# Four row blocks of W3 as halves, and batch 0 ahead of the last block: reordering the loads and the first stage of a fused retention and feed-forward kernel

## Chip, cores and metric

The kernel runs on one core of one Trainium2 chip, alone. The metric is device time in microseconds (us) of one execution. The kernel before takes 182.81 us, the median of three executions between 182.58 and 183.25. The profile is of a further execution of the same program, whose span from first to last instruction is 183.3 us; times inside it are counted from the span's start.

## What is computed

Two stages stand one behind the other. The first is a retention layer, given as a recurrence over 768 positions for 4 batches and 8 heads of width 64. The second is a feed-forward layer with a product of two projections in place of an activation.

```python
# retention: q, k, v are [4, 8, 768, 64] in float32
gamma = 1.0 - 2.0 ** (-5.0 - np.arange(H))
for t in range(S):
    state = gamma * state + outer(k[:, :, t], v[:, :, t])
    y[:, :, t] = (1 / sqrt(D)) * (q[:, :, t] @ state)
x = y.transpose(0, 2, 1, 3).reshape(B * S, H * D)      # [3072, 512]

# feed-forward: w1, w2 [512, 1024], w3 [1024, 1024], w_out [1024, 512]
h = ((x @ w1) * (x @ w2)) @ w3
out = h @ w_out                                        # [3072, 512]
```

There is nothing between the last two products, so `w3 @ w_out` can be multiplied out once, as a matrix of 1024 x 512, and each token then needs one product in place of two. The kernel does this at its start; the change is about that start.

## The kernel before, in words

**Instructions are issued in written order.** The scheduler is set to manual, so each engine executes its instructions in the order in which the Python code calls them. An instruction that waits holds up everything behind it on its own engine, and nothing on the others. There are six queues to keep in mind: TensorE (PE, with its weight loads PEld), VectorE (DVE), ScalarE (ACT), GpSimd (POOL), and SyncE (SP), from which the loads are issued by `dma_in` (line 63).

**Loads.** Every input comes in float32 into a ring of 22 staging tiles of 128 x 1024 (`new_stage`, tile name `stg`). A row block of W3, W1 or W2 is 128 rows of 4 KB (`load_rows`), a block of w_out is 128 pairs of rows (`load_wo`), and the first two chunks of q, k and v of a batch are 128 x 8 pieces of 512 bytes (`load_pairs`). All go through one queue, in this order: W3 block 0, w_out block 0, W3 1, w_out 1, W3 2, w_out 2, W3 3, w_out 3; then W3 blocks 4 to 7; then q, k, v of batch 0 and of batch 1; then W1 and W2 (four blocks each); then later chunks of q, k and v. Each of the tiles is 512 KB.

**W3 times w_out.** `W3O[f]` (f = 0 to 7) is row block f of the product. W3 block f is cast to float16 (`cast_w3`), turned by eight 128 x 128 transposes on PE (`w3_transpose`, lines 240 to 248), copied from the accumulator memory (PSUM) to `w3t[f]`, and multiplied with the eight half blocks of w_out (`WO`, cast by `cast_wo`), eight matmuls of 512 columns that add up in one PSUM bank. For blocks 0 to 3 these eight are taken in four parts of two matmuls (`w3_part(f, i)`, line 255, with i the w_out block), because w_out arrives in turn with W3; four banks are held as `acc`. Blocks 4 to 7 go through `W3Block` (line 269), whose `mm(n)` issues the next n of the eight matmuls and whose `back` copies the result out on ACT (line 276). `busy(m, n)` (line 686) issues m matmuls of n columns on zeros, whose result nobody reads; they fill time on PE.

**First batches.** `Pairs(e)` (e = 0, 1) handles the first 256 positions of batch e: casts of q, k, v, transposes of q and k, `scores`, `intra` (scores times v), `kv` (the state), `inter` (state times q), and `outputs_back` to `XT[e]`, the input of the feed-forward layer. In `v_cast` on POOL, v is scaled with decays; `YS` holds the output decays, made in `output_decays` by three multiplications on DVE and three exponentials on ACT; `masks_and_decays` makes masks and constants on POOL.

**Start of the feed-forward layer.** `by_rows(W1, ps, d, blocks)` (line 795) multiplies row block d of W1 with the first tokens; there is one group of matmuls per block d, since the blocks arrive one by one. The first of them waits for the first half cast of W1 block 0 on ACT (line 769) and, for the columns from 512 on, on POOL (line 770). The end of batch 1's retention stands between these groups. After that one step follows another for each pair of chunks, in which PE has work all the time: the feed-forward products (`Ffn.mm`, line 636, and `o_unit`, line 663) of one pair of chunks and the retention of the next.

Of the kernel before, what the change touches and what calls it, by code (L numbers as in the profile page):

```python
# [10 lines left out]
HP = mybir.dt.float16  # L11
# [7 lines left out]
def kernel(  # L19
# [11 lines left out]
    nc = tc.nc  # L31
# [39 lines left out]
    def load_q(n):  # L71

        g, e = divmod(n, 2)
        if g >= NSTEP // 2:
            return
        bp, cp = divmod(g, NCH // 2)
        q_in[n] = load_pairs(q, bp * 2 + e, cp)

    def load_pairs(src, b, cp):
        t = new_stage()  # L80
        dma_in(
            t[:, :].rearrange("p (h x) -> p h x", x=2 * D),
            src[b, :, cp * 2 * C : (cp + 1) * 2 * C, :].rearrange("h (p t) d -> p h (t d)", t=2),
        )
        return t
# [19 lines left out]
    def new_stage():  # L105
        return wstage.tile([128, 1024], FP, tag="wst", name="stg")

    def load_rows(src, i):
        t = new_stage()
        dma_in(t[:, :], src[i * 128 : (i + 1) * 128, :])  # L110
        return t

    def load_wo(i):
        t = new_stage()
        dma_in(
            t[:, :].rearrange("p (t n) -> p t n", t=2),
            moe_w_out[i * 256 : (i + 1) * 256, :].rearrange("(p t) n -> p t n", t=2),
        )
        return t

    w3_st, wo_st = [], []
    for i in range(4):
        w3_st.append(load_rows(moe_w3, i))
        wo_st.append(load_wo(i))
    for f in range(4, 8):
        w3_st.append(load_rows(moe_w3, f))
    for e in range(2):
        load_q(e)
        k_in[e] = load_pairs(k, e, 0)
        v_in[e] = load_pairs(v, e, 0)  # L130
    w1_st = [load_rows(moe_w1, d) for d in range(4)]
    w2_st = [load_rows(moe_w2, d) for d in range(4)]
    load_q(2)
# [36 lines left out]
    keep = const.tile([128, L], FP, name="keep")  # L170
    keep_t = const.tile([128, 2, 128], FP, name="keep_t")

    def masks_and_decays():

        nc.gpsimd.memset(keep[:, :], 1.0)
        for s in range(2):
            r = slice(s * L, (s + 1) * L)
            nc.gpsimd.affine_select(
                out=keep[r, :], in_=keep[r, :], compare_op=mybir.AluOpType.is_ge, fill=0.0,
                base=0, pattern=[[1, 2], [2, 32]], channel_multiplier=-1,  # L180
            )

        nc.gpsimd.memset(keep_t[:, :, :], 1.0)
        for s in range(2):
            for t in range(2):
                nc.gpsimd.affine_select(
                    out=keep_t[half(s), t, :], in_=keep_t[half(s), t, :], compare_op=mybir.AluOpType.is_ge,
                    fill=0.0, base=-t, pattern=[[1, 2], [2, 64]], channel_multiplier=-2,
                )
        for h in range(H):  # L190
            for s in range(2):
                nc.gpsimd.memset(LGP[half((h + s) % 2), s, h // 2 : h // 2 + 1], math.log(gam[h]))
        for h in range(H):
            p, r = h // 2, (h % 2) * 64
            nc.gpsimd.memset(GS[r : r + 64, p : p + 1], gam[h] ** C)

    def output_decays():
        for n, (s, swap) in enumerate(((0, 0), (1, 0), (1, 1))):
            x = fsb.tile([128, NP, L], FP, tag="pa", name="ys_x", bufs=8)
            nc.vector.tensor_tensor(  # L200
                x[:, :, :], if_f[:, s, :].unsqueeze(1).broadcast_to((128, NP, L)),
                LGP[:, swap, :].unsqueeze(2).broadcast_to((128, NP, L)), MULT,
            )
            nc.scalar.activation(YS[:, n, :, :], x[:, :, :], AF.Exp)

    mark_t = const.tile([1, 1], HP, name="mark")
    XT = {}
# [8 lines left out]
    def cast_to(dst, src, on_dve):  # L216
        if on_dve:
            nc.vector.tensor_copy(dst, src)
        else:
            nc.scalar.copy(dst, src)  # L220

    def cast_wo(i):
        dst = WO[i][:, :, :].rearrange("p a n -> p (a n)")
        nc.scalar.copy(dst[:, 0:512], wo_st[i][:, 0:512])  # L224
        nc.gpsimd.tensor_copy(dst[:, 512:1024], wo_st[i][:, 512:1024])  # L225

    def cast_w3(f):
        t = att.tile([128, 1024], HP, tag="qT", name="w3h", bufs=5)
        st = w3_st[f]
        if f < 4:  # L230
            nc.vector.tensor_copy(t[:, 0:512], st[:, 0:512])  # L231
            nc.scalar.copy(t[:, 512:1024], st[:, 512:1024])
        else:
            cast_to(t[:, :], st[:, :], f == 4)
        W3h[f] = t

    def bank(tag, shape, dtype, name):
        return ps_at.tile(shape, dtype, tag=tag, name=name)

    def w3_transpose(f):  # L240
        src, ps = W3h.pop(f), bank(("X0", "X1")[f % 2], [128, 1024], HP, "psW3")
        for g in range(8):
            c0 = (g // 2) * 256 + g % 2
            nc.tensor.transpose(  # L244
                ps[:, g * 128 : (g + 1) * 128], src[:, c0 : c0 + 255 : 2], ident16[:, :]
            )
        w3t[f] = att.tile([128, 1024], HP, tag="k16" if f < 3 else "v16", name="w3t", bufs=3)
        nc.vector.tensor_copy(w3t[f][:, :], ps[:, :])  # L248

    def w3_part(f, *parts):  # L250

        for i in parts:
            for r in range(2):
                g = i * 2 + r
                nc.tensor.matmul(  # L255
                    acc[f], lhsT=w3t[f][:, g * 128 : (g + 1) * 128], rhs=WO[i][:, r, :],
                    start=(g == 0), stop=(g == 7),
                )
            if i == 3:
                cast_to(W3O[f][:, :], acc[f], f < 3)  # L260

    class W3Block:
        def __init__(self, f):
            self.f, self.t, self.g = f, w3t.pop(f), 0
            self.ps = ps_f.tile([128, DM], FP, tag="psF", name="psW")

        def mm(self, n):
# [412 lines left out]
    def busy(m, tag="Y0", n=512):  # L680
        if tag:
            ps = bank(tag, [128, 512], FP, "psZ")
        else:
            ps = ps_f.tile([128, 512], FP, tag="psF", name="psZ")
        for _ in range(m):
            nc.tensor.matmul(ps[:, 0:n], lhsT=Z[:, 0:128], rhs=Z[:, 0:n], start=True, stop=True)  # L686

    cast_w3(0)
    busy(8)
    acc = [ps_f.tile([128, DM], FP, tag="psF", name="psW")[:, :] for _ in range(4)]  # L690
    w3_transpose(0)
    cast_wo(0)
    busy(2, n=400)
    w3_part(0, 0)
    busy(3)
    cast_w3(1)
    w3_transpose(1)
    busy(3)
    cast_wo(1)
    w3_part(0, 1)  # L700
    w3_part(1, 0, 1)
    cast_w3(2)
    w3_transpose(2)
    busy(2, n=400)
    cast_wo(2)
    w3_part(0, 2)
    w3_part(1, 2)
    w3_part(2, 0)
    cast_w3(3)
    w3_transpose(3)  # L710
    w3_part(2, 1, 2)
    cast_wo(3)
    masks_and_decays()
    cast_w3(4)
    for f in range(3):
        w3_part(f, 3)
    cast_w3(5)
    w3_part(3, 0, 1)
    w3_transpose(4)
    cast_w3(6)  # L720
    w3_part(3, 2, 3)
    w3_transpose(5)
    cast_w3(7)
    output_decays()
    wb = W3Block(4)
    wb.mm(4)
    w3_transpose(6)
    wb.mm(4)
    wb.back()
    q_cast(0, nc.gpsimd)  # L730
    wb = W3Block(5)
    wb.mm(4)
    w3_transpose(7)
    wb.mm(4)
    wb.back()
    b0, b1 = Pairs(0), Pairs(1)
    b0.k_cast(nc.vector)
    q_transposes(0, "Y0", False)
    b0.v_cast(nc.gpsimd, 0)
    b0.v_cast(nc.gpsimd, 1)  # L740
    wb = W3Block(6)
    wb.mm(4)
    b0.k_transposes("Y1", True)
    wb.mm(4)
    am_back = b0.scores(0)
    wb.back()
    am_back(0)
    am_back(1)
    wb = W3Block(7)
    wb.mm(3)  # L750
    am_back = b0.scores(1)
    am_back(0)
    b0.kv(True)
    b0.state()
    am_back(1)
    b0.intra(0)
    q_cast(1, nc.scalar, nc.gpsimd)
    wb.mm(1)
    q_transposes(1, "X0", False)
    b1.k_cast(nc.gpsimd)  # L760
    last = ended(b0.intra(1), nc.gpsimd)
    b0.outputs_back(0)
    wb.mm(1)
    b1.k_transposes(None, False, 2)
    b0.inter(last)
    b0.next_state_add()
    b0.outputs_back(1)
    b1.v_cast(nc.gpsimd, 0)
    nc.scalar.copy(W1[0][:, 0:512], w1_st[0][:, 0:512])  # L769
    nc.gpsimd.tensor_copy(W1[0][:, 512:1024], w1_st[0][:, 512:1024])  # L770
    b1.v_cast(nc.gpsimd, 1)
    wb.mm(1)
    am_back = b1.scores(0)
    am_back(0)
    am_back(1)
    wb.mm(2)
    wb.back()
    nc.scalar.copy(W1[1][:, 0:512], w1_st[1][:, 0:512])
    nc.gpsimd.tensor_copy(W1[1][:, 512:1024], w1_st[1][:, 512:1024])
    b0.next_state_decay()  # L780
# [18 lines left out]

    pa = [hold[i // 2][:, i % 2 * 512 : i % 2 * 512 + 512].rearrange("p (a n) -> p a n", a=2) for i in range(4)]  # L800
    ps = four_banks()
    by_rows(W1, ps, 0, (2, 3, 4, 5))
    am_back = b1.scores(1)
    am_back(0)
    am_back(1)
    b1.intra(0)
    by_rows(W1, ps, 0, (6, 7, 0, 1))
    by_rows(W1, ps, 1, range(4))
    b1.intra(1)
    b1.kv(False)  # L810
# [167 lines left out]
```

## Time and profile before

| Quantity | Value |
|---|---|
| time, median of three | 182.81 us |
| span of the profile | 183.3 us |
| PE busy | 174.3 us, 95% of the span |
| DVE, ACT, POOL busy | 108.7, 71.8, 71.5 us |
| matmuls on zeros (line 686) | 18, 5.9 us |
| W3O matmuls (lines 255 and 269) | 64, 7.7 + 8.6 us |
| transposes of W3 (line 244) | 64 in 8 groups of about 0.61 us |
| loads through SyncE's queue | 89.9% of 16 engines' span |

The profile has a table of busy time by engine, a strip of 40 slices that shows the busy tenths of each engine and the rate of the loads, a chain that is followed back from the last instruction to whatever released each step, and groups of instructions by line. The trace behind it can also be asked for a timeline of one engine, for the waits by engine and line, and for busy time and load rate in chosen stretches. In a timeline the columns are start, duration, engine, line, operation and tiles, count, and in brackets the idle time of the engine just before with what ended it. A line `SPq L63` is the issue of a load; a load lands several us later, and its landing is seen by the reader as the end of a wait that is put down to `DMA`.

### The profile page before, as it was taken

To read this page: it belongs to the slowest core of one execution; us is meant where nothing else is said; L and a number is where in the kernel's file an instruction comes from. 1 tells how busy PE (TensorE), PEld (TensorE's weight loads), DVE (VectorE), ACT (ScalarE), POOL (GpSimd) and SP (SyncE) were. 2 spreads that over 40 slices of the span, in tenths; PEclk is the share of its full clock that TensorE was granted. 3 is DMA by queue.
4 is the path that set the end of the run, shared out by engine and by line. 5 is a ranking of instruction groups with operands and counts; after the bars stand their busy time and mean duration, and the time that the engine had idled before them with its cause. 6 is when DMAs were issued, how large, how long until landed. Compare 5 with 4: busy or idle time off the path is not lost.

```text
span 183.3 us, 6222 instructions
## 1 busy us (share of the span) xinstructions
PE 174.3 (95%) x2634; PEld 124.7 (68%) x2634; DVE 108.7 (59%) x204; ACT 71.8 (39%) x157; POOL 71.5 (39%) x127
## 2 busy tenths in 40 slices
PE   7689999799999999999999999999999999999992
PEld 2345646588766696785876858758678587685871
DVE  2247658670769678648468484395685865845430
ACT  4353844455630332433333424334244242342531
POOL 3127526864547650824416364037450260000000
PEclk9999999999999999999999999999999999999999
DMA  5999999999999989999999999999999930200203
GB/s 215 344 418 404 299 273 288 368 401 278 215 260 234 174 254 221 221 283 223 213 212 175 322 192 239 207 191 290 225 149 250 159 114 7 114 0 29 89 0 114
DMA packets 79530, 39.71 MB, mean 217 GB/s; under 512 B 57360, under 2 KB 74000, under 8 KB 79504
## 3 DMA queue, kind: packets, MB, share of 16 engines
q1 hardware_dynamic: 79072, 38.81, 89.9%
q8 instruction: 20, 0.33, 0.8%
q10 hardware_dynamic: 432, 0.52, 0.8%
q14 instruction: 6, 0.05, 0.1%
HBM read 29.36 MB, written 6.29 MB: 195 GB/s over the span
## 4 chain that ended last, share of the span: by engine, by line
PE 78%; SPq 9%; DMA 9%; ACT 1%; issue 1%; ACTq 0%
PE psF L636 40%; PE psO L663 23%; SPq L63 9%; DMA stg<-in_moe_w_out_dram 5%; DMA stg<-in_moe_w_dram 4%; PE psF L795 4%; PE psY L531 2%; PE psY L599 2%; PE psA L383 2%; PE psG L636 2%; PE psK L551 1%; PE psTk L357 1%; ACT w L220 1%; PE psTq L328 0%; ACT osb L667 0%
## 5 line engine op out<-in xcount | busy, mean ns | idle before, releaser
L636 PE MATMUL psF<-xt,w 128*128 128x256 f16 x672 | 76.5, 273 | 0.0
L636 PEld LDWEIGHTS <-w 128*128 128x128 f16 x704 | 68.4, 98 | 10.3
L651 DVE TENSOR_TENSOR ht<-pa,psF 128x256 f16<-128x256 f32 x88 | 36.9, 420 | 37.6 <-PE psF L636 31.6
L663 PE MATMUL psO<-w3o,ht 128*128 128x512 f16 (+2 forms) x200 | 44.0, 371 | 0.3 <-issue 0.3
L645 ACT COPY pa<-psF 128x256 f32<-128x256 f32 x80 | 29.7, 371 | 37.1 <-PE psF L636 37.1
L663 PEld LDWEIGHTS <-ht 128*128 128x128 f16 x200 | 18.5, 98 | 19.9 <-issue 0.6
L667 ACT ACTIVATE osb<-psO 128x512 f32<-128x512 f32 (+2 forms) x25 | 14.5, 580 | 44.4 <-PE psO L663 44.4
L614 DVE TENSOR_TENSOR xt<-psY,YS 64x512 f16<-64x512 f32 (+1 forms) x29 | 21.1, 728 | 5.2 <-PE psY L599 4.8
L310 POOL TENSOR_TENSOR v<-stg,VS 128x512 f16<-128x512 f32 x20 | 20.6, 1042 | 5.1 <-DMA stg<-in_v_dram 5.0
L303 POOL CAST k<-stg 128x512 f16<-128x512 f32 x18 | 11.0, 612 | 25.3 <-DMA stg<-in_k_dram 25.1
L290 POOL CAST q<-stg 128x1024 f16<-128x1024 f32 (+1 forms) x12 | 12.0, 1003 | 15.3 <-DMA stg<-in_q_dram 10.8
L390 DVE TENSOR_TENSOR am<-psA,keep 128x512 f16<-128x512 f32 x20 | 12.8, 680 | 0.6 <-PE psA L383 0.6
L566 POOL TENSOR_TENSOR t<-s,GS 128x512 f16<-128x512 f32 x8 | 8.3, 1040 | 12.3 <-DVE s L565 12.3
L795 PE MATMUL psF<-xt,w 128*128 128x256 f16 x64 | 8.3, 273 | 1.1 <-ACT w L769 1.0
L255 PE MATMUL psW<-wo,w3t 128*128 128x512 f16 x32 | 7.7, 379 | 1.0 <-ACT wo L224 1.0
L269 PE MATMUL psW<-wo,w3t 128*128 128x512 f16 x32 | 8.6, 381 | 0.0
L248 DVE COPY w3t<-psW 128x1024 f16<-128x1024 f16 x8 | 5.5, 688 | 4.9 <-PE psW L244 4.9
L795 PEld LDWEIGHTS <-w 128*128 128x128 f16 x64 | 5.9, 98 | 2.7 <-ACT w L769 1.5
L686 PE MATMUL psZ<-zeros 128*128 128x512 f16 (+1 forms) x18 | 5.9, 461 | 1.3 <-DVE zeros L143 1.3
L244 PEld LDWEIGHTS <-w3h 128*128 128x128 f16 x64 | 4.1, 98 | 3.7 <-DVE w3h L231 2.3
L573 DVE TENSOR_TENSOR t<-psK,t 128x512 f16<-128x512 f32 x9 | 6.2, 690 | 0.6 <-PE psK L551 0.5
L225 POOL CAST wo<-stg 128x512 f16<-128x512 f32 x4 | 2.4, 612 | 10.2 <-DMA stg<-in_moe_w_out_dram 10.2
(92 smaller groups left out, 148.1 us busy)
## 6 DMA issues: line engine op xcount, KB each, us to landing
stg<-in_moe_w_dram SPq DMA_DIRECT2D x16, 512.0 KB, 9.3
stg<-in_q_dram SPq DMA_DIRECT2D x12, 512.0 KB, 6.3
out_dram<-osb SPq DMA_DIRECT2D x22, 256.0 KB, 3.5
stg<-in_k_dram SPq DMA_DIRECT2D x20, 256.0 KB, 5.7
stg<-in_v_dram SPq DMA_DIRECT2D x20, 256.0 KB, 5.8
stg<-in_moe_w_out_dram SPq DMA_DIRECT2D x4, 512.0 KB, 7.8
stg<-in_k_dram SPq DMA_DIRECT2D x2, 512.0 KB, 10.5
stg<-in_v_dram SPq DMA_DIRECT2D x2, 512.0 KB, 8.8
```

Of the source, the lines that this page charges most:

```text
L63: nc.sync.dma_start(dst, src)
L290: (nc.scalar.copy if eng is nc.scalar else eng.tensor_copy)(dst[:, :].rearrange("i (t h d) -> i h t d", t=2, d=D)[:, hs, :, :], src[:, :]. ...
L303: (nc.scalar.copy if eng is nc.scalar else eng.tensor_copy)(dst, src)
L310: eng.tensor_tensor(v16[:, e, :].rearrange("j (h d) -> j h d", d=D), v32[:, e, :].rearrange("j (h d) -> j h d", d=D), VS[:, 2, :].unsqueez ...
L390: nc.vector.tensor_tensor(am[:, r, :, :], ps[r][:, :, :], keep[:, :].unsqueeze(1).broadcast_to((128, NP * 2, L)), MULT,)
L614: nc.vector.tensor_tensor(XT[m][to, :, s, :].rearrange("p (a e) (i t) -> p a e t i", e=2, t=2), psYs[m][s][fr, :, :].rearrange("p (a e) (t ...
L636: nc.tensor.matmul(ps[:, :], lhsT=W[d][:, f * 128 : (f + 1) * 128], rhs=self.x(d), start=(d == 0), stop=(d == 3),)
L645: nc.scalar.copy(self.pa[f][:, :], ps[:, :])
L651: nc.vector.tensor_tensor(self.HT[:, f, :], self.pa.pop(f)[:, :], ps[:, :], MULT)
L663: nc.tensor.matmul(psO[:, :], lhsT=self.HT[:, f, e * 128 : (e + 1) * 128], rhs=W3O[f][:, cs], start=(f == 0), stop=(f == 7),)
L667: nc.scalar.activation(osb[:, cs], psO[:, :], AF.Copy, scale=final_scale)
L795: nc.tensor.matmul(ps[f // 2][:, f % 2, :], lhsT=W[d][:, f * 128 : (f + 1) * 128], rhs=f0.x(d), start=(d == 0 and f % 2 == 0), stop=(d == ...
```

## The change

**Loads.** W3 blocks 0 to 3 are loaded as two column halves of 256 KB each, with rows of 2 KB (`load_w3(f, h)`). The order becomes: W3 0 left, w_out 0, W3 1, 2, 3 left, w_out 1, W3 0 right, w_out 2, W3 1, 2, 3 right, w_out 3, W3 4 to 6, then q, k, v of batch 0, then W3 7, then q, k, v of batch 1. Everything after that is unchanged. The left half of a W3 block is what its parts 0 and 1 need.

**Casts and transposes by halves.** `cast_half(f, h)` casts the left half on DVE and the right half on ACT, in separate places of the program; `w3_transpose(f, h=...)` makes four transposes and one copy to `w3t`. For blocks 0 to 3, transposes of a block now stand ahead of matmuls of earlier blocks, so that their copies run beside those matmuls. Block 4 is cast in halves on DVE and ACT, blocks 5 to 7 on ACT. The copy of an `acc` bank is no longer in `w3_part` but in `w3_back`.

**Small work.** `masks_and_decays` is split into `masks` and `decays`. The three multiplications of `output_decays` go from DVE to POOL (`output_decays_x`); the exponentials stay on ACT. The matmuls on zeros become 26 of 256 columns.

**Order of the rest.** Batch 0's transposes and scores stand between the matmuls of blocks 5 and 6; block 7 is transposed inside batch 0's retention, with a bank of the other pool and its copy on ACT, and its eight matmuls stand around the k transposes and first scores of batch 1. The first group of `by_rows` takes column blocks 2, 3, 0, 1 and the second 4 to 7, so that the first needs only the half of W1 block 0 that ACT casts.

Its purpose is to give PE real work earlier while the loads come in, and to keep copies out of the way of the matmuls. The diff, cut to what matters:

```diff
-    for i in range(4):
-        w3_st.append(load_rows(moe_w3, i))
-        wo_st.append(load_wo(i))
-    for f in range(4, 8):
-        w3_st.append(load_rows(moe_w3, f))
-    for e in range(2):
-        load_q(e)
-        k_in[e] = load_pairs(k, e, 0)
-        v_in[e] = load_pairs(v, e, 0)
+    def load_w3(f, h):
+        if f not in w3_st:
+            w3_st[f] = new_stage()
+        cs = slice(h * 512, h * 512 + 512)
+        dma_in(w3_st[f][:, cs], moe_w3[f * 128 : (f + 1) * 128, cs])
+    for x in ((0, 0), "o0", (1, 0), (2, 0), (3, 0), "o1", (0, 1), "o2", (1, 1), (2, 1), (3, 1), "o3"):
+        if x[0] == "o":
+            wo_st[int(x[1])] = load_wo(int(x[1]))
+        else:
+            load_w3(*x)
+    for f in (4, 5, 6):
+        w3_st[f] = load_rows(moe_w3, f)
+    load_q(0)
+    k_in[0] = load_pairs(k, 0, 0)
+    v_in[0] = load_pairs(v, 0, 0)
+    w3_st[7] = load_rows(moe_w3, 7)
+    load_q(1)
+    k_in[1] = load_pairs(k, 1, 0)
+    v_in[1] = load_pairs(v, 1, 0)
...
-            nc.vector.tensor_tensor(
+            nc.gpsimd.tensor_tensor(
                 x[:, :, :], if_f[:, s, :].unsqueeze(1).broadcast_to((128, NP, L)),
...
+    def cast_half(f, h):
+        cast_w3(f, nc.scalar if h else nc.vector, cols=(h * 512, h * 512 + 512))
...
-    cast_w3(0)
-    busy(8)
+    cast_half(0, 0)
+    busy(12, n=256)
...
+    w3_transpose(0, h=0)
     cast_wo(0)
-    busy(2, n=400)
+    busy(6, n=256)
+    cast_half(1, 0)
     w3_part(0, 0)
-    busy(3)
-    cast_w3(1)
-    w3_transpose(1)
-    busy(3)
+    w3_transpose(1, h=0)
+    busy(2, n=256)
+    cast_half(2, 0)
+    w3_transpose(2, h=0)
+    w3_part(1, 0)
+    cast_half(3, 0)
+    busy(2, n=256)
+    w3_transpose(3, h=0)
+    w3_part(2, 0)
     cast_wo(1)
...
+    cast_w3(7, nc.scalar)
     wb.back()
     b0.v_cast(nc.gpsimd, 0)
     b0.v_cast(nc.gpsimd, 1)
...
     b0.intra(0)
     q_cast(1, nc.scalar, nc.gpsimd)
-    wb.mm(1)
+    w3_transpose(7, True, False)
+    b0.kv(True)
+    b0.state()
+    b1.k_cast(nc.gpsimd)
+    last = ended(b0.intra(1), nc.vector)
+    b0.outputs_back(0)
     q_transposes(1, "X0", False)
...
+    wb = W3Block(7)
+    wb.mm(4)
+    b1.k_transposes(None, False, 2)
+    wb.mm(3)
     b1.v_cast(nc.gpsimd, 0)
...
     am_back = b1.scores(0)
     am_back(0)
     am_back(1)
-    wb.mm(2)
+    wb.mm(1)
+    nc.scalar.copy(W1[0][:, 0:512], w1_st[0][:, 0:512])
+    nc.gpsimd.tensor_copy(W1[0][:, 512:1024], w1_st[0][:, 512:1024])
     wb.back()
+    b1.v_cast(nc.gpsimd, 1)
...
-    by_rows(W1, ps, 0, (2, 3, 4, 5))
+    by_rows(W1, ps, 0, (2, 3, 0, 1))
     am_back = b1.scores(1)
...
-    by_rows(W1, ps, 0, (6, 7, 0, 1))
+    by_rows(W1, ps, 0, (4, 5, 6, 7))
```

More of the change, by code (lines that the diff above doesn't have):

```diff
@@ L119, in load_wo @@
         return t
-    w3_st, wo_st = [], []
-    for i in range(4):
-        w3_st.append(load_rows(moe_w3, i))
-        wo_st.append(load_wo(i))
-    for f in range(4, 8):
-        w3_st.append(load_rows(moe_w3, f))
-    for e in range(2):
-        load_q(e)
-        k_in[e] = load_pairs(k, e, 0)
-        v_in[e] = load_pairs(v, e, 0)
+    w3_st, wo_st = {}, {}
+    def load_w3(f, h):
[17 more added lines that the diff above has]
+    v_in[1] = load_pairs(v, 1, 0)
     w1_st = [load_rows(moe_w1, d) for d in range(4)]
@@ L171, with masks @@
     keep_t = const.tile([128, 2, 128], FP, name="keep_t")
-    def masks_and_decays():
+    def masks():
         nc.gpsimd.memset(keep[:, :], 1.0)
@@ L189, in masks_and_decays, with decays @@
                 )
+    def decays():
         for h in range(H):
@@ L195, in masks_and_decays, with output_decays_x @@
             nc.gpsimd.memset(GS[r : r + 64, p : p + 1], gam[h] ** C)
-    def output_decays():
-        for n, (s, swap) in enumerate(((0, 0), (1, 0), (1, 1))):
+    ys_x = []
+    def output_decays_x():
+        for s, swap in ((0, 0), (1, 0), (1, 1)):
             x = fsb.tile([128, NP, L], FP, tag="pa", name="ys_x", bufs=8)
-            nc.vector.tensor_tensor(
+            nc.gpsimd.tensor_tensor(
                 x[:, :, :], if_f[:, s, :].unsqueeze(1).broadcast_to((128, NP, L)),
@@ L203, in output_decays @@
             )
-            nc.scalar.activation(YS[:, n, :, :], x[:, :, :], AF.Exp)
+            ys_x.append(x)
+    def output_decays():
+        for n in range(3):
+            nc.scalar.activation(YS[:, n, :, :], ys_x[n][:, :, :], AF.Exp)
     mark_t = const.tile([1, 1], HP, name="mark")
@@ L225, in cast_wo, with cast_w3, w3_transpose @@
         nc.gpsimd.tensor_copy(dst[:, 512:1024], wo_st[i][:, 512:1024])
[L227 to L235, printed above, removed]
+    def cast_w3(f, *engs, cols=(0, 1024)):
+        if f not in W3h:
+            W3h[f] = att.tile([128, 1024], HP, tag="qT", name="w3h", bufs=5)
+        n = (cols[1] - cols[0]) // len(engs)
+        for i, eng in enumerate(engs):
+            cs = slice(cols[0] + i * n, cols[0] + i * n + n)
+            (nc.scalar.copy if eng is nc.scalar else eng.tensor_copy)(W3h[f][:, cs], w3_st[f][:, cs])
+    def cast_half(f, h):
+        cast_w3(f, nc.scalar if h else nc.vector, cols=(h * 512, h * 512 + 512))
     def bank(tag, shape, dtype, name):
         return ps_at.tile(shape, dtype, tag=tag, name=name)
-    def w3_transpose(f):
-        src, ps = W3h.pop(f), bank(("X0", "X1")[f % 2], [128, 1024], HP, "psW3")
-        for g in range(8):
+    banks_used = []
+    def w3_transpose(f, psf=False, on_dve=True, h=None):
+        gs = range(8) if h is None else range(h * 4, h * 4 + 4)
+        if psf:
+            ps = ps_f.tile([128, 1024], HP, tag="psF", name="psW3")
+        else:
+            ps = bank(("X0", "X1")[len(banks_used) % 2], [128, 1024], HP, "psW3")
+            banks_used.append(f)
+        for g in gs:
             c0 = (g // 2) * 256 + g % 2
             nc.tensor.transpose(
-                ps[:, g * 128 : (g + 1) * 128], src[:, c0 : c0 + 255 : 2], ident16[:, :]
+                ps[:, g * 128 : (g + 1) * 128], W3h[f][:, c0 : c0 + 255 : 2], ident16[:, :]
             )
-        w3t[f] = att.tile([128, 1024], HP, tag="k16" if f < 3 else "v16", name="w3t", bufs=3)
-        nc.vector.tensor_copy(w3t[f][:, :], ps[:, :])
+        if f not in w3t:
+            w3t[f] = att.tile([128, 1024], HP, tag=("k16", "v16")[f in (1, 3, 5, 7)], name="w3t", bufs=3)
+        cs = slice(gs[0] * 128, gs[-1] * 128 + 128)
+        cast_to(w3t[f][:, cs], ps[:, cs], on_dve)
     def w3_part(f, *parts):
@@ L258, in w3_part, with w3_back @@
                 )
-            if i == 3:
-                cast_to(W3O[f][:, :], acc[f], f < 3)
+    def w3_back(f, on_dve):
+        cast_to(W3O[f][:, :], acc[f], on_dve)
     class W3Block:
         def __init__(self, f):
-            self.f, self.t, self.g = f, w3t.pop(f), 0
+            self.f, self.t, self.g = f, w3t[f], 0
             self.ps = ps_f.tile([128, DM], FP, tag="psF", name="psW")
@@ L686, in busy @@
             nc.tensor.matmul(ps[:, 0:n], lhsT=Z[:, 0:128], rhs=Z[:, 0:n], start=True, stop=True)
-    cast_w3(0)
-    busy(8)
+    cast_half(0, 0)
+    busy(12, n=256)
     acc = [ps_f.tile([128, DM], FP, tag="psF", name="psW")[:, :] for _ in range(4)]
-    w3_transpose(0)
+    w3_transpose(0, h=0)
     cast_wo(0)
-    busy(2, n=400)
+    busy(6, n=256)
+    cast_half(1, 0)
     w3_part(0, 0)
-    busy(3)
-    cast_w3(1)
-    w3_transpose(1)
-    busy(3)
+    w3_transpose(1, h=0)
+    busy(2, n=256)
@@ L699 @@
+    cast_half(2, 0)
[5 more added lines that the diff above has]
+    w3_part(2, 0)
     cast_wo(1)
+    cast_half(0, 1)
+    busy(2, n=256)
+    w3_part(3, 0)
+    busy(1, n=256)
     w3_part(0, 1)
[L701 to L704, printed above, removed]
+    w3_part(1, 1)
+    w3_transpose(0, h=1)
+    w3_part(2, 1)
     cast_wo(2)
+    masks()
+    for f in range(1, 4):
+        cast_half(f, 1)
+    w3_part(3, 1)
@@ L706 @@
+    busy(1, n=256)
+    w3_transpose(1, h=1)
     w3_part(0, 2)
+    w3_transpose(2, h=1)
     w3_part(1, 2)
[L708 to L711, printed above, removed]
+    w3_transpose(3, h=1)
     cast_wo(3)
[L713 to L718, printed above, removed]
-    w3_transpose(4)
-    cast_w3(6)
-    w3_part(3, 2, 3)
+    decays()
+    output_decays_x()
+    w3_part(2, 2)
+    w3_part(3, 2)
+    cast_w3(4, nc.vector, nc.scalar)
@@ L722 @@
+    w3_part(0, 3)
+    w3_back(0, False)
+    w3_part(1, 3)
+    w3_part(2, 3)
+    w3_transpose(4)
+    cast_w3(5, nc.scalar)
+    w3_back(1, True)
+    w3_part(3, 3)
+    wb = W3Block(4)
+    wb.mm(2)
     w3_transpose(5)
-    cast_w3(7)
+    w3_back(2, True)
+    w3_back(3, False)
+    cast_w3(6, nc.scalar)
+    wb.mm(6)
     output_decays()
-    wb = W3Block(4)
+    wb.back()
+    q_cast(0, nc.gpsimd)
+    b0, b1 = Pairs(0), Pairs(1)
+    wb = W3Block(5)
     wb.mm(4)
     w3_transpose(6)
+    b0.k_cast(nc.vector)
@@ L728 @@
     wb.mm(4)
     wb.back()
-    q_cast(0, nc.gpsimd)
-    wb = W3Block(5)
+    q_transposes(0, "Y0", False)
+    wb = W3Block(6)
+    wb.mm(1)
+    b0.k_transposes("Y1", True)
+    wb.mm(3)
+    am_back = b0.scores(0)
+    am_back(0)
+    am_back(1)
     wb.mm(4)
-    w3_transpose(7)
-    wb.mm(4)
+    cast_w3(7, nc.scalar)
     wb.back()
-    b0, b1 = Pairs(0), Pairs(1)
-    b0.k_cast(nc.vector)
-    q_transposes(0, "Y0", False)
     b0.v_cast(nc.gpsimd, 0)
     b0.v_cast(nc.gpsimd, 1)
-    wb = W3Block(6)
@@ L742 @@
[L742 to L750, printed above, removed]
     am_back = b0.scores(1)
     am_back(0)
-    b0.kv(True)
-    b0.state()
     am_back(1)
@@ L757 @@
     q_cast(1, nc.scalar, nc.gpsimd)
-    wb.mm(1)
-    q_transposes(1, "X0", False)
[L760 to L764, printed above, removed]
+    w3_transpose(7, True, False)
[4 more added lines that the diff above has]
+    b0.outputs_back(0)
+    q_transposes(1, "X0", False)
     b0.inter(last)
@@ L767 @@
     b0.outputs_back(1)
+    wb = W3Block(7)
+    wb.mm(4)
+    b1.k_transposes(None, False, 2)
+    wb.mm(3)
     b1.v_cast(nc.gpsimd, 0)
[L769 to L772, printed above, removed]
     am_back = b1.scores(0)
@@ L775 @@
     am_back(1)
-    wb.mm(2)
+    wb.mm(1)
+    nc.scalar.copy(W1[0][:, 0:512], w1_st[0][:, 0:512])
+    nc.gpsimd.tensor_copy(W1[0][:, 512:1024], w1_st[0][:, 512:1024])
     wb.back()
+    b1.v_cast(nc.gpsimd, 1)
     nc.scalar.copy(W1[1][:, 0:512], w1_st[1][:, 0:512])
```

## The prediction, made before the changed kernel was run

> **What bounds the kernel now.** I read the page's strip first, to see where PE is not full; then the chain of waits over the first 50 us, to see what sets the moment from which PE is full; then PE's timeline around that moment, and the load rate by stretches.
>
> The chain, in order of time (start, duration, what):
>
> ```profile
> 11.83 3.81 SPq L63
> 15.69 3.68 SPq L63
> ...
> 23.95 1.99 SPq L63
> 25.94 0.04 issue
> 25.98 7.30 DMA stg<-in_moe_w_dram
> 33.28 0.02 issue
> 33.31 0.63 ACT w L769
> 33.93 0.05 issue
> 33.98 0.61 PE psF L795 x4
> ```
>
> Up to 33.3 us the chain holds hardly anything but the load queue. It ends with the landing of W1 block 0; ACT casts half of it in 0.63 us, and the first matmul of the feed-forward layer starts at 33.98. From there the chain is almost PE alone. PE's timeline around that moment:
>
> ```profile
> 32.41 0.60 PE L269 MATMUL psW<-wo,w3t 128*128 128x512 f16 x2
> 33.98 0.61 PE L795 MATMUL psF<-xt,w 128*128 128x256 f16 x4 [0.97 <-ACT w L769]
> ```
>
> PE had finished everything else at 33.01 and stood idle for 0.97 us. Busy time by stretches (start:end and length, then busy us and count of PE, PEld, DVE, ACT, POOL, then clock, load share and GB/s):
>
> ```profile
> 5.00:8.00 3.00, 1.82 (x12) 0.58 (x9) 0.72 (x2) 0.65 (x2) 0.61 (x1) 1.00 0.96 335
> 8.00:15.00 7.00, 6.00 (x45) 3.39 (x46) 3.19 (x6) 3.67 (x6) 1.80 (x4) 1.00 1.02 414
> 15.00:18.50 3.50, 3.50 (x24) 1.82 (x22) 2.96 (x6) 1.25 (x3) 3.01 (x18) 1.00 1.03 399
> 22.00:25.50 3.50, 3.29 (x34) 2.03 (x32) 1.38 (x2) 1.70 (x3) 0.49 (x1) 1.00 1.12 282
> 26.00:31.50 5.50, 5.27 (x126) 3.21 (x126) 4.22 (x8) 2.30 (x4) 3.86 (x6) 1.00 0.97 273
> 34.00:38.00 4.00, 4.00 (x106) 2.85 (x107) 2.27 (x5) 1.65 (x3) 3.67 (x5) 1.00 1.02 407
> 50.00:181.00 131.00, 129.28 (x2118) 96.31 (x2115) 82.49 (x156) 45.43 (x113) 46.68 (x53) 1.00 0.89 180
> ```
>
> The loads never rest: about 414 GB/s with rows of 4 KB, 282 with pieces of 512 bytes. PE is full after 34 us, with 1.7 us of 131 idle between 50 and 181. So the time is: landing of W1 block 0, plus its cast, plus a PE tail of 183.3 - 34.0 = 149.3 us that the change doesn't touch. An earlier finish of W3 is worth something only if it makes that first matmul start earlier.
>
> One more view, DVE's casts of W3 blocks 0 to 3, with the wait ahead of each:
>
> ```profile
> 4.13 0.43 DVE L231 CAST w3h<-stg 128x512 f16<-128x512 f32 x1 [1.40 <-DMA stg<-in_moe_w_dram]
> ...
> 7.97 0.43 DVE L231 CAST w3h<-stg 128x512 f16<-128x512 f32 x1 [2.01 <-DMA stg<-in_moe_w_dram]
> ...
> 10.56 0.43 DVE L231 CAST w3h<-stg 128x512 f16<-128x512 f32 x1 [0.75 <-DMA stg<-in_moe_w_dram]
> ...
> 13.11 0.43 DVE L231 CAST w3h<-stg 128x512 f16<-128x512 f32 x1 [0.55 <-DMA stg<-in_moe_w_dram]
> ```
>
> Two blocks of 512 KB lie between consecutive casts: 2.55 to 2.59 us in the regular case, so 1.28 us a block, but 3.84 us the first time. The loads lost about 1.27 us between 4 and 8 us and never made it up.
>
> **What the Trainium skill says.** In "DMA: Bandwidth & Descriptors", the section on why a DMA increments its semaphore by 16 says that a load is spread over up to 16 engines that finish independently, and is complete when the last has counted. So one engine that is late delays every later landing while the others run ahead. The trace fits: 335 GB/s instead of 414 over 3 us is 0.57 us of loads on average, while the landings slipped 1.27 us. The same page, in the table of measured bandwidth, gives some 10.5 ns per packet as a floor; the trace gives nearly the same, below. "TensorE: Matmul & The Clock Gate", in "What's actually happening", says that PE runs at half rate until it has been busy for a window of some 3.4 us. The trace agrees in the durations, though its clock column shows 1.00 throughout: the first eight matmuls of 512 columns take 3.28 us, 410 ns each, and fourteen later ones 3.19 us, 228 each.
>
> **The change, part by part.**
>
> Bytes ahead of W1 block 0: the same 18 tiles, in another order, so nothing is gained there. What is added is packets. From the stretches: a packet of 4 KB costs one of 16 engines 16 x 4096 B / 414 GB/s = 158 ns, one of 512 bytes 16 x 512 / 282 = 29 ns. The line through both has 10.6 ns per packet besides its bytes. Four blocks in halves are 4 x 128 = 512 more packets, 32 per engine, 0.34 us. No load with 2 KB rows is in the trace; if neighbouring packets overlap, the cost is 0. I take 0.2 us. All of it is ahead of W1 block 0: +0.2 on the path. Four more issues at about 0.44 us each on SyncE cost nothing: twelve take 5.5 us while their 4 MB take over 10 to land.
>
> PE's early work: 32 `w3_part` matmuls and the 64 transposes are the same. The left halves let parts 0 and 1 of all four blocks (16 matmuls, 3.5 us at 216 ns) run by about 10 us, where the kernel before has done 8 by 11.4. So PE gets ahead by some 8 x 0.216 = 1.7 us. Fillers were 5.9 us and are now 12 x 0.21 cold and 14 x 0.11 warm, 4.1 us, in time when PE waits for loads. All this ends up as longer idling before 33.98: worth 0 at the end.
>
> Batch 0 ahead of W3 block 7: q, k, v of batch 0 land 1.28 us earlier (q about 20.3 for 21.4, v about 25.1 for 26.2), block 7 about 6.6 us later, at 26.4. Batch 1's q, k, v keep their places (+0.2). After batch 0, PE's queue has block 7's transposes, which wait for its cast on ACT (26.4 + 1.05 = 27.4), and behind them `kv`, `intra` and everything of batch 1. By then PE comes from `intra(0)`, which needs v (25.1 + 1.04 on POOL) and the masked scores, about 27.5 to 27.9: nearly no wait. Then kv 0.5, intra 0.5, q transposes 0.6, inter 0.4: about 30.4; four matmuls of block 7, 0.9: 31.3. Batch 1's k lands at 29.9, is cast by 30.9, transposed by 31.8, copied to the first half by 32.3; scores and four matmuls of block 7 end at about 33.1. W1's cast ends at 33.3 + 0.2 + 0.6 = 34.1. Slack 1.0 us, about the 0.97 of before: 0.
>
> ACT from 26.4 on: cast of block 7 1.05, a W3O copy 0.6, half of q 0.6, copy of block 7's transposes 1.0, qT 1.0, kT 1.1: 5.3 us in the 7.1 until W1 lands. It hides.
>
> POOL: three products of 128 x 256, by the row of line 490 0.61 each, 1.8 us (with 0.8 each, 2.4). Masks (2.8 us, 14.98 to 17.8 before) move ahead of w_out 3, into the wait there; the decays (2.3) and the three products then end at about 19.5, ahead of q at 20.3. DVE loses 1.1 us. Both hidden.
>
> `by_rows` in the order 2, 3, 0, 1 needs ACT's cast only (ends 33.93 before); POOL's ended at 33.95. Worth 0.02.
>
> Sum: +0.2 for packets, 0 for the rest: 182.81 + 0.2 = 183.0.
>
> **The rivals.**
>
> A, the loads don't lose their 1.27 us, or the change escapes part of it. It struck in the stretch whose loads are now cut differently. Then W1 block 0 lands at 33.3 - 1.27 + 0.2 = 32.2. The kernel before could have used only 0.97 of that, PE being full from 12.5 to 33.0; the new order, 1.7 us ahead on W3, could use all: 182.81 - 1.07 = 181.7. For it: an irregular loss needn't recur. Against it: the same queue runs full over the same bytes, and whatever held some engines may do so again.
>
> B, batch 1 comes late to the first `by_rows`, because block 7 now stands whole behind batch 0. If block 7 lands a us later and its cast and copy queue behind other ACT work, another us is lost; of 2.0 us the slack eats 1.0: 183.0 + 1.0 = 184.0. For it: PE executes in order, and kv and intra stand behind block 7's transposes. Against it: ACT is busy for 2.3 us of the 5.5 between 26 and 31.5.
>
> C, the loads lose more: the late engine meets an instruction fetch as well. The page has 20 of these of 16 KB, 0.33 MB on the q8 queue; at a per-engine rate of 414/16 = 26 GB/s one costs an engine 0.63 us, and double that if it shares with loads. W1 lands 1.0 later: 184.0.
>
> D, the aim of the change works and PE was the bound: the 0.97 us of idling and no more, 181.8. Against it: ACT waited 0.81 us for the landing before line 769. I count it with A.
>
> **How the numbers follow.** The case that nothing moves but the packets gets 0.43 and gives the predicted time. Faster by over 0.5% (below 181.9) comes from A and D, 0.32; slower (above 183.7) from B, 0.15, and C, 0.10. The range goes from A's 181.7, less 0.1 for PE waits that vanish elsewhere, to B's and C's 184.0 plus 0.2 for unknown packet and ACT costs: 181.6 to 184.2.
>
> **What would show it.** Right: ACT's cast of W1 block 0 still waits for a load and starts at 33.3 to 33.7; PE idles 1 us or more just ahead of the first line 795 group; PE idles more before 33 us than the 4.8 us of before; the tail from that matmul to the end stays at 149.3. Wrong: that cast starts below 32.6 (A), or PE comes to the group after the cast is done (B), or the gap between the first landings shrinks or grows (A, C), or the tail itself changes, which no step here allows for.

## The result and the profile after

The changed kernel takes 185.51 us, median of three between 185.26 and 186.06, where 182.81 was measured before: a ratio of 1.0149, interval 1.0102 to 1.0196. It is slower; 183.0 us, 0.2 us more than before, had been forecast. A second set on one chip, taken for the experiments, gave 1.0101 (1.0044 to 1.0157). So the change costs 1.0 to 1.5%, about 1.9 to 2.7 us. Some executions of every kernel here are slower than the rest, and those more than 1.5% above their kernel's fastest are left out of the ratios.

The page after, its first line and the strips of PE and of PE's clock:

```profile
span 183.4 us, 6250 instructions
...
PE   7499999899999999999999999999999999999992
...
PEclk9879999999999999999999999999999999999999
```

and the same two strips before:

```profile
PE   7689999799999999999999999999999999999992
...
PEclk9999999999999999999999999999999999999999
```

The span is that of the profile before, 183.3, within 0.1 us. The two profiles shown first can't explain a difference of 2 us; why will be seen in E5. In the second slice PE's strip falls to 4, where it had 6 before, and its clock is below full in the second and third, which it wasn't before. Pieces of the loading stage in the chain of waits after (start, duration, what), and its end:

```profile
13.36 5.73 SPq L63
...
26.45 7.71 DMA stg<-in_moe_w_dram
34.17 0.02 issue
34.19 0.63 ACT w L827
34.82 0.04 issue
34.86 0.61 PE psF L848 x4
```

and PE's timeline after at the same place:

```profile
33.24 0.42 PE L463 MATMUL psA<-qT,kT 64*64 64x128 f16 x16
33.59 0.39 PE L303 MATMUL psW<-wo,w3t 128*128 128x512 f16 x1
34.86 0.61 PE L848 MATMUL psF<-xt,w 128*128 128x256 f16 x4 [0.88 <-ACT w L827]
```

It is the picture of before, 0.88 us later: PE is done with everything else and waits for the cast of W1 block 0, which waits for the load. Line 848 is the former 795, and 827 the former 769. Busy time by stretches after, in the columns used for the kernel before:

```profile
3.50:5.00 1.50, 1.47 (x12) 0.89 (x11) 0.75 (x2) 0.00 (x0) 0.00 (x0) 1.00 0.83 274
5.00:8.00 3.00, 0.92 (x8) 0.36 (x6) 0.53 (x2) 0.62 (x1) 0.61 (x1) 1.00 0.99 363
8.00:15.00 7.00, 6.58 (x44) 3.60 (x44) 2.68 (x6) 3.72 (x6) 3.19 (x10) 0.76 1.01 385
14.00:18.00 4.00, 3.91 (x28) 2.06 (x27) 2.03 (x5) 1.86 (x3) 3.05 (x25) 1.00 1.02 403
```

Between 3.5 and 5 us the queue is busy for 0.83 of the time and moves 274 GB/s. PE is busy for 0.92 us of the three from 5 to 8, and after that hole its clock is granted at 0.76 on average.

### The profile page after: what moved, and what is told of

Read it like the earlier page. It is cut to its first block, busy times and chain, and to the rows that moved or that the text cites. A ratio compares the mean times of both kernels' runs of the same rounds, so it can differ in the third digit from the quotient of the medians.

```text
span 183.4 us, 6250 instructions
## 1 busy us (share of the span) xinstructions
PE 174.4 (95%) x2642; PEld 125.9 (69%) x2642; DVE 106.9 (58%) x204; ACT 74.1 (40%) x160; POOL 72.8 (40%) x129
## 4 chain that ended last, share of the span: by engine, by line
PE 78%; DMA 11%; SPq 7%; ACT 1%; issue 0%; ACTq 0%
PE psF L670 40%; PE psO L697 23%; DMA stg<-in_moe_w_dram 8%; SPq L63 7%; PE psF L848 4%; DMA stg<-in_moe_w_out_dram 3%; PE psY L565 2%; PE psA L417 2%; PE psY L633 2%; PE psG L670 2%; PE psK L585 1%; PE psTk L391 1%; ACT w L242 1%; PE psTq L362 0%; ACT osb L701 0%
## 5 line engine op out<-in xcount | busy, mean ns | idle before, releaser
L288 PE MATMUL psW<-wo,w3t 128*128 128x512 f16 x32 | 9.2, 397 | 2.2 <-ACT wo L246 2.1
L240 DVE COPY w3t<-psW 128x512 f16<-128x512 f16 (+1 forms) x11 | 5.5, 498 | 9.8 <-PE psW L275 9.8
L303 PE MATMUL psW<-wo,w3t 128*128 128x512 f16 x32 | 8.4, 380 | 0.4 <-DVE w3t L240 0.4
L720 PE MATMUL psZ<-zeros 128*128 128x256 f16 x26 | 5.9, 368 | 1.3 <-DVE zeros L157 1.3
L470 DVE TENSOR_TENSOR am<-psA,keep_t 128x512 f16<-128x512 f32 x8 | 5.2, 686 | 3.0 <-PE psA L463 2.9
L255 ACT CAST w3h<-stg 128x512 f16<-128x512 f32 (+1 forms) x8 | 6.2, 780 | 1.3 <-DMA stg<-in_moe_w_dram 0.7
```

## Experiments

Each ratio is to executions of the kernel before on the same chip in the same set. Three theories are in play at first. L: the landing of W1 block 0 sets the time, as forecast, and the new loads make it late (P is its form in the first four expectations). O: the new order of work costs PE time. M: there is no real difference. F, K and S were formed after the first four experiments.

**E1, the changed kernel again**, beside the next three.

> The changed kernel once more, timed beside the kernel before. Theory P (the loads land later: 512 more packets and a stall in the first loads put the landing of W1 block 0 from 33.28 to 34.17 us, and the tail behind it is unchanged): slower by about 0.9 us, ratio near 1.005. Theory O (the new order costs PE time after the landing too): slower by 2.7 us as in the first timing, ratio 1.015. Theory M (the profiled spans, 183.3 before and 183.4 after, are the truth and the 2.7 us come from how the two sets of executions were taken): ratio within 0.5% of 1.

1.0101 (1.0044 to 1.0157): the interval leaves out 1, so M falls as a claim of no difference. P's 1.005 and O's 1.015 both lie within it, so it doesn't decide between these. The profiled execution took 185.46 us. ACT's cast of W1 block 0 and PE's first matmul of W1, from two timelines of E1:

```profile
34.05 0.62 ACT L827 CAST w<-stg 128x512 f16<-128x512 f32 x1 [1.00 <-DMA stg<-in_moe_w_dram]
```

```profile
34.72 0.61 PE L848 MATMUL psF<-xt,w 128*128 128x256 f16 x4 [1.37 <-ACT w L827]
```

Three of its stretches, with the slow start and yet a full clock:

```profile
3.50:5.00 1.50, 1.43 (x10) 0.82 (x9) 0.71 (x2) 0.01 (x1) 0.00 (x0) 1.00 0.79 259
5.00:8.00 3.00, 2.19 (x13) 1.00 (x11) 1.13 (x4) 0.61 (x1) 0.61 (x1) 1.00 0.98 354
8.00:15.00 7.00, 6.54 (x50) 3.64 (x50) 2.85 (x8) 4.04 (x7) 3.46 (x11) 1.00 1.02 389
```

**E2, halves alone**, in the kernel before.

```diff
-        w3_st.append(load_rows(moe_w3, i))
+        w3_st.append(new_stage())
+        for h in range(2):
+            cs = slice(h * 512, h * 512 + 512)
+            dma_in(w3_st[i][:, cs], moe_w3[i * 128 : (i + 1) * 128, cs])
```

> The kernel before, with each of W3 blocks 0 to 3 loaded as two column halves one directly after the other; nothing else. P: W1 block 0 lands 0.3 to 0.9 us later than before (33.6 to 34.2 us) and the time grows by as much. O: W1 lands at most 0.3 later, time within 0.3 us of before. M: no change in time.

1.0014 (0.9985 to 1.0043), which doesn't show a cost in time. Its trace does show the slow start: 251 GB/s from 3.5 to 5 us, and PE's clock at 0.76 between 8 and 15. PE's first W1 matmul:

```profile
34.57 0.61 PE L798 MATMUL psF<-xt,w 128*128 128x256 f16 x4
```

That is as late as in the changed kernel, but not for P's reason. Nothing waits for W1 block 0, which GpSimd casts at 33.32 us without a wait; it is PE's own work that comes to this point late, after a wait that ended with the landing of w_out block 0 at 7.87 us.

**E3, the changed kernel with whole blocks.** Loads as before up to w_out 3; the order of the matmuls stays.

```diff
-    for x in ((0, 0), "o0", (1, 0), (2, 0), (3, 0), "o1", (0, 1), "o2", (1, 1), (2, 1), (3, 1), "o3"):
...
+    for i in range(4):
+        w3_st[i] = load_rows(moe_w3, i)
+        wo_st[i] = load_wo(i)
```

> The changed kernel, with W3 blocks 0 to 3 loaded whole and alternating with w_out as before; its order of casts, transposes and matmuls stays. P: W1 block 0 lands at 33.3 as before, the time comes back to that of before, within 0.3 us. O: stays as slow as the changed kernel. M: same as before, as everything here.

1.0235 (1.0168 to 1.0301), slower still, so P's time failed. Its landing came true: GpSimd's cast of W1 block 0 waits for the load and starts at 32.85 us, within the range of before. But PE arrives late, and the first W1 matmul starts at 36.46 us. The new order takes the left halves of all four blocks first, and with whole blocks in turn with w_out PE is busy for 4.79 us of the seven from 8 to 15, against 6.54 in E1. So the time doesn't separate the loads from the order: the order needs the halves.

**E4, W3 block 7 ahead of batch 0 again**, in the changed kernel.

```diff
-    for f in (4, 5, 6):
+    for f in (4, 5, 6, 7):
...
-    w3_st[7] = load_rows(moe_w3, 7)
```

> The changed kernel, with W3 block 7 loaded ahead of batch 0's q, k and v as before. P: no different from the changed kernel, W1 block 0 at about 34.2. O: faster than the changed kernel by most of what it lost. M: same as before.

1.0117 (1.0091 to 1.0143): as slow as the changed kernel. Putting batch 0 ahead of block 7 isn't where the time goes. The first W1 matmul starts at 34.77 us here, behind a cast on ACT that waits for no load.

**E5, the kernel before again.** Theory F: TensorE's fetches of instructions hold up the late load engine. Theory K: the fall of the clock is the cost.

> The kernel before, unchanged, for a second profile of it: its executions lie between 182.4 and 187.6 us and the profile shown first is of one of 185. Theory F (TensorE's second instruction fetch of 16 KB decides: where it comes before W1 block 0 has landed, it holds up the load engine that is already late by about 1.1 us): the fetch again starts at about the time of the first line 795 matmul or later, and W1 block 0 lands at 31.5 to 33.3 us. Theory K (TensorE's clock falls back in the first 15 us and costs the time): a full clock from 5 us on in a fast execution.

1.0000 (0.9963 to 1.0037). Its profiled execution took 183.25 us, with a span of 181.5. The first profile of before was of an execution of 184.97 us, above the median of 182.81. Cast and first W1 matmul in E5:

```profile
32.52 0.62 ACT L769 CAST w<-stg 128x512 f16<-128x512 f32 x1 [0.82 <-DMA stg<-in_moe_w_dram]
```

```profile
33.19 0.61 PE L795 MATMUL psF<-xt,w 128*128 128x256 f16 x4 [0.97 <-ACT w L769]
```

Against E1 the W1 matmuls start 1.53 us earlier. The stretches of E5:

```profile
3.50:5.00 1.50, 1.50 (x8) 0.52 (x7) 0.43 (x1) 0.62 (x1) 0.00 (x0) 1.00 1.00 396
5.00:8.00 3.00, 2.88 (x14) 1.14 (x12) 1.01 (x2) 0.94 (x2) 0.61 (x1) 1.00 0.98 392
8.00:15.00 7.00, 6.44 (x47) 3.49 (x47) 3.04 (x6) 3.38 (x6) 2.03 (x5) 1.00 1.03 415
14.00:18.00 4.00, 4.00 (x27) 2.05 (x25) 3.31 (x6) 1.66 (x2) 3.43 (x14) 1.00 1.02 401
```

396 GB/s from 3.5 to 5 us, where the changed kernel had 274 and E1 259; PE busy for 2.88 us of the next three, where they had 0.92 and 2.19; and a full clock, as in E1.

The fall of the clock, K, is not what costs the time. In E14 (below) ten executions have a mean clock of 0.981 to 0.991 and ten of 0.997 or more; their mean times are 184.85 and 184.79 us. In E2 it is eleven and eleven, with 184.65 and 184.35 us. So it is worth some 0.3 us or less here.

E5 against E1 accounts for the difference of their executions, each a little below its kernel's median, 185.46 - 183.25 = 2.21 us: 34.72 - 33.19 = 1.53 in the start of the W1 matmuls; (183.4 - 34.72) - (181.5 - 33.19) = 0.37 in the tail, where PE has one gap of 0.36 us at 59.6 us with no releaser shown; and 2.06 - 1.75 = 0.31 by which the execution exceeds the span.

**E6, wider fillers**, in the changed kernel: half as many, of 512 columns.

```diff
-    busy(12, n=256)
+    busy(6)
...
-    busy(6, n=256)
+    busy(3)
...
-    busy(2, n=256)
+    busy(1)
```

> The changed kernel with its filling matmuls of 256 columns in pairs made into half as many of 512 columns: the same filling time, 12 matmuls (24 instructions of TensorE) fewer ahead of W1. F: the second fetch moves behind the landing of W1 block 0, which lands about 1.1 us earlier than in the changed kernel (34.1), and most of the 1% comes back: ratio 1.000 to 1.005. K: no different from the changed kernel, ratio 1.010 to 1.015.

1.0077 (1.0052 to 1.0102): between the two, and overlapping the changed kernel. The landing is at 33.52 us in its profile. F fails in its own terms: up to 32 us, ahead of every landing concerned, there are two instruction fetches on the q8 queue in E5 as in E1 and the changed kernel, so their number ahead of the landing isn't what differs.

**E7, narrower fillers**, in the kernel before.

```diff
-    busy(8)
+    busy(16, n=256)
```

> The kernel before with its first 8 filling matmuls of 512 columns made into 16 of 256: the same filling time, 16 instructions more. F: the second fetch comes ahead of W1's landing and the time grows by 0.5 to 1.1 us, ratio 1.003 to 1.006. K: no difference.

1.0056 (1.0032 to 1.0079), the number that F gave, but not for its reason: the cast of W1 block 0 starts at 31.90 us, earlier than in any other profile of the kernel before. PE then has gaps later: 0.78 us at 49.25 us, where it waits for ACT's cast of a k, and a larger one at a line 663 matmul (PE's timeline of E7):

```profile
59.65 2.54 PE L663 MATMUL psO<-w3o,ht 128*128 128x512 f16 x11 [1.24 <-issue]
```

"issue" means that nothing in the profile shows what PE waited for. The changed kernel has 0.23 us at that place, E1 0.36, E5 none. Its cause is open.

**E8, output decays back on VectorE**, in the changed kernel.

```diff
-            nc.gpsimd.tensor_tensor(
+            nc.vector.tensor_tensor(
                 x[:, :, :], if_f[:, s, :].unsqueeze(1).broadcast_to((128, NP, L)),
...
-    output_decays_x()
...
+    output_decays_x()
     output_decays()
     wb.back()
```

> The changed kernel with the three products for the output decays back on VectorE, just ahead of their exponentials. F: no different from the changed kernel (ratio 1.010 to 1.015). Theory S (work moved to GpSimd, and with it the 0.4 us by which an execution of the changed kernel exceeds its span more than one of before does): faster than the changed kernel by 0.4 us or more.

1.0085 (1.0062 to 1.0108), which overlaps the changed kernel's interval: S's 0.4 us isn't shown in the time. The execution exceeds the span by 184.90 - 183.1 = 1.80 us, for 2.06 in E1.

**E10, the same products moved the other way**, in the kernel before.

```diff
-            nc.vector.tensor_tensor(
+            nc.gpsimd.tensor_tensor(
                 x[:, :, :], if_f[:, s, :].unsqueeze(1).broadcast_to((128, NP, L)),
```

> The kernel before with the three products for the output decays on GpSimd in place of VectorE, nothing else. Theory S (these products cost 0.35 us outside the span: executions exceed their spans by 2.06 to 2.13 us in the changed kernel, by 1.67 to 1.75 before, and by 1.80 with the products back on VectorE): execution minus span is 2.0 to 2.1 us, time up by 0.2%. Against S: it stays at 1.7.

184.19 - 182.1 = 2.09 us outside the span, for 1.67 and 1.75 before. It is so in every execution: 2.01 to 2.12 us in all 20 of this kernel, 1.66 to 1.78 in all 59 of before beside them. S is right that these products bring some 0.35 us that no engine row shows (E13, without them, has 1.75 to 1.84, so about 0.1 us can have other causes). The ratio, 1.0011 (0.9982 to 1.0040), allows that as a cost in time and can't prove it.

**E9, halves by rows**, in the kernel before: 64 rows of 4 KB each.

```diff
+            dma_in(w3_st[i][h * 64 : h * 64 + 64, :], moe_w3[i * 128 + h * 64 : i * 128 + h * 64 + 64, :])
```

> The kernel before with W3 blocks 0 to 3 loaded as two halves by rows: 64 rows of 4 KB each, so twice as many loads but packets as large as before. If it is the number and size of loads that slows the queue between 3.5 and 8 us (250 to 280 GB/s with column halves, 374 to 407 without): the rate is low here too and W1 block 0 lands later than before. If it is the packets of 2 KB: rate and landing as before (32.5 us).

1.0195 (1.0123 to 1.0267). It tells nothing about the packets, since loads of 64 partitions were slow even with rows of 4 KB: about 220 GB/s from 2 to 5 us and 303 from 8 to 11. Why is open.

**E11, W1 block 0 loaded ahead of batch 1's v**, in the changed kernel.

```diff
+    w1_st = [load_rows(moe_w1, 0)]
     v_in[1] = load_pairs(v, 1, 0)
-    w1_st = [load_rows(moe_w1, d) for d in range(4)]
+    w1_st += [load_rows(moe_w1, d) for d in range(1, 4)]
```

> The changed kernel with W1 block 0 loaded ahead of batch 1's v. Theory L (the landing of W1 block 0 is what the changed kernel waits for; it comes 1.3 to 1.6 us later than in a typical execution before): the wait of 0.9 to 1.4 us ahead of the first line 848 matmul goes, and the kernel becomes 0.5 to 1.0 us faster, ratio 1.005 to 1.010 in place of 1.010 to 1.015. Against L (the new order of the matmuls itself costs the time): no change.

1.0069 (1.0043 to 1.0095), for 1.0101 to 1.0149 without it. This is the number that L gave, but the intervals overlap, so a gain isn't clear of noise. PE's timeline of E11:

```profile
33.88 0.61 PE L849 MATMUL psF<-xt,w 128*128 128x256 f16 x4 [0.27 <-ACT w L828]
```

The start moved from 34.72 to 33.88 us. It isn't bound by the load of W1 any more: PE's own work comes to this point only at 33.61. So the late landing accounts for a part of the loss, and PE's work, nearly as late, keeps the rest.

**E12, the same in the kernel before**, with GpSimd's half of W1 block 0 cast ahead of v.

```diff
+        if e == 1:
+            w1_st = [load_rows(moe_w1, 0)]
         v_in[e] = load_pairs(v, e, 0)
...
-    b1.v_cast(nc.gpsimd, 0)
     nc.scalar.copy(W1[0][:, 0:512], w1_st[0][:, 0:512])
     nc.gpsimd.tensor_copy(W1[0][:, 512:1024], w1_st[0][:, 512:1024])
+    b1.v_cast(nc.gpsimd, 0)
```

> The kernel before with W1 block 0 loaded ahead of batch 1's v, and its GpSimd half cast ahead of that v's. L: the wait of 0.97 us ahead of the first line 795 matmul goes, and the kernel is up to 0.9 us faster than before, ratio 0.995 to 1.000. Against L: no change or slower, since v of batch 1 lands 1.3 us later and intra needs it.

0.9967 (0.9936 to 0.9998): the only version here whose interval lies below 1, and narrowly. In its trace PE goes on to the W1 matmuls without a wait:

```profile
32.77 0.61 PE L797 MATMUL psF<-xt,w 128*128 128x256 f16 x4
```

The same move leaves the changed kernel (E11) some 1% behind: its first W1 matmul comes 1.11 us later than here, with no wait for the load of W1 in either.

**E13, late halves**: in the kernel before, W3 blocks 4 to 7 as column halves and 0 to 3 whole; the edit is E2's, in the other loop.

> The kernel before with W3 blocks 4 to 7, not 0 to 3, loaded as two column halves each. If the cost is a steady one of the packets: the rate between 14 and 18 us falls from about 412 to 370 GB/s or less and everything behind lands about 0.9 us later, as with the halves of blocks 0 to 3. If it is the start: the rate is 390 to 415 GB/s there, the cost at most 0.4 us.

0.9981 (0.9952 to 1.0011): no cost is shown. The stretch with the halves, in E13:

```profile
14.00:18.00 4.00, 4.00 (x30) 2.11 (x27) 3.02 (x5) 1.60 (x2) 3.29 (x16) 1.00 1.05 389
```

389 GB/s for 401 in E5 and 407 in the first profile: 2.1 MB take 0.16 to 0.24 us longer.

**E14, early halves only**: in the kernel before, W3 blocks 0 and 1 as column halves, with E2's edit.

> The kernel before with W3 blocks 0 and 1 alone loaded as two column halves each. If the cost is a steady one of the packets: half of that of four blocks, about 0.45 us by the landing of w_out block 3. If it is the start: the rate between 3.5 and 5 us is again 250 to 280 GB/s and w_out block 3 lands 0.6 to 0.9 us later than in the kernel before.

1.0059 (1.0034 to 1.0084), with half the small packets of E13. Its stretches:

```profile
3.50:5.00 1.50, 1.19 (x8) 0.49 (x6) 0.43 (x1) 0.00 (x0) 0.00 (x0) 1.00 1.01 228
5.00:8.00 3.00, 0.74 (x6) 0.43 (x7) 0.69 (x1) 1.13 (x2) 0.48 (x1) 0.89 0.99 337
8.00:15.00 7.00, 6.84 (x39) 3.52 (x39) 2.48 (x5) 3.20 (x6) 1.35 (x3) 0.80 1.02 414
```

The queue is slow at the start alone, and from 8 us on it is back at 414 GB/s. So it isn't the packets as such but where they stand. Between 3.5 and 5 us the loads ran at 366 to 407 GB/s in the six profiles with the order of before and whole early blocks (before, E5, E7, E10, E12, E13), and at 228 to 280 in the eight with early column halves (the changed kernel, E1, E2, E4, E6, E8, E11, E14). The landing of w_out block 3, read at ACT's cast of it, sums that up: 13.37 to 14.59 us in the six, 14.65 to 15.77 in the eight. The means are 14.18 and 15.14, about 0.95 us apart. As in E2, the first W1 matmul (33.76 us) waits for no load: W1 block 0 has landed by 32.93, when GpSimd casts it.

## Why the prediction was wrong, by its own steps

**What bounds the kernel: right, but with a second path close behind.** In the changed kernel (its two profiles, E6 and E8) the landing of W1 block 0, its cast and a PE tail set the time. E12's gain fits that; E11's isn't clear of noise. PE's own work, though, came to W1 only at 33.98 us in the changed kernel's profile, at 33.35 in E1 and at 33.61 in E11. With the landing alone put right, 0.9 to 1.4 us at most could come back in the first two.

**Packets, +0.2 us on the path: the term that failed.** Its working assumed a full queue throughout. For a full queue it is about right: E13 paid some 0.2 us for as many packets. At the start it is not: early halves put the landing of w_out block 3 off by 0.95 us on average. What the term stood for, the delay of the first W1 matmul, came to 1.3 us: it starts at 34.20 to 34.86 us in five profiles with the changed order of loads (the changed kernel, E1, E4, E6, E8), and at 32.57 to 33.98 in five of before (the first, E5, E7, E10, E13).

How the slow start becomes these 1.3 us is only in part shown. W1 block 0 is cast from 33.52 to 34.19 us on in those five, and at 31.90 to 33.31 in the five of before. With whole early blocks in the changed kernel it lands by 32.85 (E3), so there the halves seem to be what makes it late. With halves alone in the kernel before it lands by 33.3 and 32.9 (E2, E14), no later than in some profiles without; there it is PE's work that comes late.

**Early PE work, 1.7 us ahead and worth 0: wrong in the lead.** Parts 0 and 1 of all four blocks were to be done by about 10 us; they were done at 13.1 in E1 and 14.8 in the changed kernel's profile, since the first loads landed late. PE came to W1 later than before (33.01 and, in E5, 32.22), not earlier. Idle time between 5 and 8 us was followed by a fall of the clock in the profiles of five of the eight kernels with early halves (the changed one, E2, E4, E8, E14) and in E9, and in none of the six with the order of before and whole early blocks. In the changed kernel this is hidden behind the landing of W1, and E1, with a full clock, is as slow.

**Everything else at 0: right inside the span, wrong outside it.** In the changed kernel PE was done ahead of W1's cast with 0.88 and 1.37 us to spare, about the slack forecast, so rival B, block 7 in the way of batch 1, falls; E4 says the same. The products on GpSimd were hidden, as forecast, and yet add about 0.3 us to an execution, outside its span (E8, E10). No step allowed for that.

Added up, 1.3 us at the first W1 matmul and 0.3 outside the span make some 1.6 of the 1.9 to 2.7 us; the rest isn't assigned.

**Tail of 149.3 us: right within its scatter.** It is 148.5 in the changed kernel's profile, 148.7 in E1 and 148.3 in E5; E7, with its gaps, has 150.7.

**The rivals.** A and D, the faster ones, did not come. C had the right direction and nearly the size, loads that lose more; its cause, a further instruction fetch, was not shown (E6).

**The base.** The 182.81 us and the profile belonged to different executions, and the profile's, 184.97, lies above its kernel's median. The loss of 1.27 us between 4 and 8 us, which the prediction read from it and rival A called irregular, isn't what sets it apart: with 3.84 us there, the first two casts of W3 lie 3.51 to 3.93 us apart in five of the six profiles with the order of before and whole early blocks, and only in E7 2.74. So the loss is the rule, and A's premise was wrong.

Open: why halves at the start slow the queue at all; which part of the 1.3 us is due to the order of the loads and of the work rather than to the halves, since no run here gives the new order both the halves that it needs and a fast start; and why E2, with more halves than E14, shows no cost in time, though their intervals overlap. That one late load engine holds up the landings, as the prediction argued, isn't shown either: the views here give the mean of all 16.

## What to carry to other kernels

Find the landing that releases the long dense stage, and ask of every edit whether it moves that landing; then ask what comes to the same point just behind it. Be wary of cutting the first loads of a kernel into small ones in order to start sooner: here that slowed the start of the queue, and the same cut in mid-stream showed no cost. To gain, try putting the load that releases the dense stage ahead of one whose data is needed after it (E12).

Before explaining a difference of a per cent by two profiles, compare each profile's own execution with its kernel's median.

## What was not expected of the hardware

Three GpSimd products of 128 x 256 in float32, hidden within the span, go with executions that exceed their span by 2.01 to 2.12 us in place of 1.66 to 1.78 (E10). First loads of 128 half rows of 2 KB ran at 228 to 280 GB/s between 3.5 and 5 us, where whole rows of 4 KB reached 366 to 407; later in the stream such halves ran at 389 (E13) and whole rows at 401 and 407. Loads of 64 partitions ran at about 220 GB/s early on. With PE busy for only 0.74 to 1.37 us of the three from 5 to 8, its clock from 8 to 15 us was 0.76 to 0.80 on average (the changed kernel, E2, E4, E8, E14); with 1.44 us busy in E6 it stayed full, and with 1.46 in E9 it fell to 0.76.
